# Products in eight small TensorE tiles in the last stages of a gated S4D and spectral mix

## The chip, the cores and the metric

The kernel runs on one core of a Trainium2 chip. The metric is device time in microseconds (us), the median of several executions. PE is TensorE (PEld its weight loads), DVE is VectorE, ACT is ScalarE, POOL is GpSimd, SP is SyncE.

## The reference

For an input `x` of 2048 rows (time) and 640 channels it computes a gate `g` per row and mixes two branches with it:

```
g = sigmoid((x * gate_w).sum(-1))
a = irfft(rfft(x^T, 2L) * rfft(K, 2L))[:L]^T + x * D_skip     # S4D: K from A, C, dt by exponentials
b = irfft2(rfft2(x) * (w_r + 1j * w_i))                        # spectral filter over rows and channels
out = g * a + (1 - g) * b
```

`K[d, l] = 2 Re sum_n C[d, n] exp(A[d, n] dt[d] l)`, with 128 states for each of the 640 channels.

## The kernel before

All transforms are products with tables on TensorE, in float32. The transform over 4096 points (2048 rows and as many zeros) is done in two stages, of 64 and of 64 points; channels are in four blocks `c` of 160.

- `phase_p` and `phase_b` make the kernel `K`: exponentials and sines on ACT, products on DVE and POOL, sums over the states on PE (`p_k`, L693, tiles of 128 rows and 32 columns), result in `k_d`.
- `phase_a` transforms `x`: `stage1` (L335, result `t1`) and `stage2` (L348), result in `u_d`. Beside it sums `x * gate_w` on PE; at its end DVE spreads the sums from PSUM into `T.gate` (L441), with one partition for each of 128 positions and 16 columns. The second half of `phase_a` takes the even frequencies through the spectral filter (lines 447 to 600: `fo`, `xx`, `mm`, `p_eo`, with `ue` loaded from `u_d`) and leaves the result in `s3e_d`.
- `phase_c` and `phase_d` transform `K` (`stage1` in `first`, `stage2` in `fronts`), multiply with `u_d` (`ma`, `mb`, `t2`: L795 to L801), transform back a first time (`backs`, `p_i`, L814) and store to `s3_d`.
- The last stages, also in `phase_d`, transform back a second time and mix. `last_e(c, a)` multiplies the rows from `s3e_d` (`t3e`, loaded by `load_e`) with the table `e3e` and scales with `1 - g` into `oe` (L876). `last_c(c, a)` multiplies the rows from `s3_d` (`t3`, loaded by `load_c`) with `e3`, scales with `g` and adds `oe` (for `c < 3` a multiply on DVE, L898, and an add on POOL, L899; for `c == 3` one instruction on DVE for each of the output rows, L896), and stores to `out`. `a` is 0 or 8: a group of `AG = 8` of the 16 columns of positions, so there are 8 groups of each kind. I call the work of one call a group.

In both, a group is cut into 3, 3 and 2 columns of 160 channels. Each piece takes two matmuls of 128 rows and 64 columns, one to each half of PSUM's partitions (`halved`, or the loop in `last_c`):

```
for i in (0, 64):
    nc.tensor.matmul(out[i:i + 64], w[:, i:i + 64], x, start=True, stop=True)
```

The tables hold zeros: `e3` has two copies of a 64 x 32 table on its diagonal, `e3e` has four of a 32 x 32 table.

The order is written out by hand. `merge` takes from several generators so that what they `yield`, divided by each stream's weight, grows together. In `phase_d`, for block `c` and `g` from 0 to 4, the streams are `mains` (`fronts` of one group of frequencies and `backs` of an earlier one, weight 4.8), `last_e(c, ...)` or `last_c(c - 1, ...)` (weight 2.4 each) and `first` of the next block (2.1). So `last_e(c)` runs in `g` 1 and 2 (2 and 3 for `c = 0`), `last_c(c - 1)` in `g` 3 and 4 for `c` 1 and 2; `last_c(2)` and `last_c(3)` run after the loop. `behind(T.mm)` sets the products behind the last matmul of `backs` on PE. [...]

Of the kernel before, what the change touches and what calls it, by code (L numbers as in the profile page):

```python
# [17 lines left out]
L = 2048  # L18
D = 640
# [31 lines left out]
def _tables():  # L51
# [11 lines left out]
    e1 = e1.reshape(2, 128, 128)  # L63

    kr = kr[:32].reshape(64, 32)
    e3 = np.zeros((64, 2, 2, 32))
    for j in range(2):
        e3[:, j, j, :] = kr

    e3e = np.zeros((32, 4, 4, 32))  # L70
    for r in range(4):
        e3e[:, r, JR[r], :] = kr[32:64]
    one = np.tile(np.eye(32), (4, 1))
    c1 = np.concatenate([
        e1[0], e1[1], e3.reshape(4, 32, 64).swapaxes(0, 1).reshape(128, 64), e3e.reshape(128, 128), np.eye(128), one,
        np.repeat([-1.0, 1.0], 64)[:, None], np.repeat([1.0, -1.0], 64)[:, None],
        np.full((128, 1), HALF_PI)], 1)

# [67 lines left out]


def _lay_back(y):
    y = y.reshape(4, 2, 2, 32, 16, 160)
    return np.ascontiguousarray(y.transpose(3, 2, 1, 4, 0, 5).reshape(1, L, D))  # L150


class Ctx:
    pass


def halved(nc, out, w, x):

    for i in (0, 64):
        nc.tensor.matmul(out[i:i + 64], w[:, i:i + 64], x, start=True, stop=True)  # L160


def merge(*streams):
# [20 lines left out]
def body(tc, A, out):  # L184
    nc = tc.nc
    T = Ctx()
    with ExitStack() as top:
        dram = top.enter_context(tc.tile_pool(name="dram", bufs=1, space=DRAM))
        T.u_d = dram.tile([4, 128, 17, 2, 160], F32, name="u_d")
        T.s3e_d = dram.tile([4, 32, 64, 160], F32, name="s3e_d")  # L190
        T.s3_d = dram.tile([4, 64, 64, 160], F32, name="s3_d")
        T.k_d = dram.tile([4, 128, 40, 64], F32, name="k_d")
        T.par_d = dram.tile([8, 16, 8, 5, N], F32, name="par_d")
        cst = top.enter_context(tc.tile_pool(name="cst", bufs=1))
        c1 = cst.tile([128, A["t_c1"].shape[1]], F32, name="c1")
# [10 lines left out]
        T.e3, T.e3e, T.id, T.one = take(64), take(128), take(128), take(32)  # L206
# [146 lines left out]
def phase_a(tc, A, T):  # L353
# [3 lines left out]
    with ExitStack() as ctx:  # L357
# [79 lines left out]
        V.tensor_reduce(out=lr[:, :], in_=lg.rearrange("p x a -> p a x"), axis=mybir.AxisListType.X, op=ALU.add)  # L437
        for r in range(4):
            P.matmul(p[32 * r:32 * r + 32, :], T.one, lr[:, :], start=True, stop=True)
        for r, x in enumerate((slice(31, 15, -1), slice(32, 48), slice(15, None, -1), slice(48, 64))):  # L440
            V.tensor_copy(T.gate[32 * r:32 * r + 32, 0, :], p[32 * r:32 * r + 32, x])  # L441


    with ExitStack() as ctx:
# [321 lines left out]
def phase_d(tc, A, T, ctx, out):  # L766
# [6 lines left out]
    o4 = ctx.enter_context(tc.tile_pool(name="d_o", reuse_waits="tile", bufs=4))  # L773
    dk = ctx.enter_context(tc.tile_pool(name="d_wk", reuse_waits="tile", bufs=1))
    o2 = ctx.enter_context(tc.tile_pool(name="d_o2", reuse_waits="tile", bufs=2))
    ps = ctx.enter_context(tc.tile_pool(name="c_ps", reuse_waits="tile", bufs=3, space=PSUM))
    pd = ctx.enter_context(tc.tile_pool(name="d_ps", reuse_waits="tile", bufs=2, space=PSUM))

    def load(c, g0, gn, st):
        nl = st.nl = 128 if g0 < 16 else 64  # L780
# [56 lines left out]
        while len(late) > (1 if i > 15 else 2):  # L837
            yield from backs(*late[0], sts.pop(late.pop(0)))

    def gate(i, a, n):  # L840
        return T.gate[:, i, a:a + n].unsqueeze(2).broadcast_to([128, n, 160])

    with tc.issue_after(T.trig.ins):
        S.activation(T.gate[:, 1, :], T.gate[:, 0, :], AF.Sigmoid, scale=-1.0)
# [6 lines left out]

    def load_e(c):
        t3es[c] = dk.tile([128, 16, 160], F32, tag="t3e", name="t3e")
        nc.sync.dma_start(t3es[c][:, :, :], T.s3e_d[c].rearrange("k (r a) d -> (k r) a d", r=4))

    def load_c(c, p, n, parts=1, eng=nc.sync):

# [4 lines left out]
        w = 16 // parts  # L862
        for y in range(p // 16, (p + n) // 16):
            src = T.s3_d[c, 16 * y:16 * y + 16].rearrange("k (j x a) d -> (k j) x a d", x=2, j=2)
            for a in range(0, 16, w):
                T.ld = eng.dma_start(t3s[c][y::4, :, a:a + w], src[:, :, a:a + w])

    def last_e(c, a):

        oe = oes[c, a] = o4.tile([128, AG, 160], F32, tag="oe", name="oe")  # L870
        for i in range(0, AG, 3):
            n = min(3, AG - i)
            p = pd.tile([128, 3, 160], F32, tag="pd", name="p_e")
            with behind(T.mm):
                halved(nc, p[:, 0:n], T.e3e, t3es[c][:, a + i:a + i + n])
            V.tensor_tensor(out=oe[:, i:i + n], in0=p[:, 0:n], in1=gate(1, a + i, n), op=ALU.mult)  # L876
            yield 0.8

    held = []

    def last_c(c, a):
# [6 lines left out]
        for i in range(0, AG, 3):  # L888
            n = min(3, AG - i)
            p = pd.tile([128, 3, 160], F32, tag="pd", name="p_c")  # L890
            with behind(T.mm):
                for x in range(2):
                    P.matmul(p[64 * x:64 * x + 64, 0:n], T.e3, t3[:, x, a + i:a + i + n], start=True, stop=True)  # L893
            if c == 3:
                for j in range(n):
                    V.scalar_tensor_tensor(out=ot[:, i + j], in0=p[:, j], scalar=T.gate[:, 0, a + i + j:a + i + j + 1], in1=oe[:, i + j], op0=ALU.mult, op1=ALU.add)  # L896
# [3 lines left out]
            if c < 2 and i + n == AG:  # L900
                G.dma_start(out[c, :, a:a + AG], ot[:, :, :])
            elif c == 3 and i + n > (5 if a else 6):
                x = i if a and i > 3 else 0
                nc.sync.dma_start(out[c, :, a + x:a + i + n], ot[:, x:i + n])
            yield 0.8
        if c == 2:
            held.append((out[c, :, a:a + AG], ot))

# [69 lines left out]
```

## Time and profile before

| | |
|---|---|
| median of 3 runs | 605.25 us (603.96 to 610.56) |
| profiled execution | 608.74 us, its span 607.0 us, granted clock 0.966 |
| PE busy | 535.8 us, 88% |
| DVE busy | 500.2 us, 82% |
| ACT busy | 364.8 us, 60% |
| POOL busy | 267.0 us, 44% |
| DMA | 101.98 MB, mean 168 GB/s |
| `p_e` (L160), `p_c` (L893) | 96 MATMUL records each |

Busy time is the time in which an engine had at least one instruction under way; the ends of matmuls are modelled. In the chain that ended last, each step goes back to what released it. In the view by stage, a row gives for each engine its busy time and number of instructions in that stretch. A window of the timeline merges instructions of one line that follow each other: start, length, count.

### The profile page before, as it was taken

The numbers are of one execution on the slowest core, as the hardware profiler recorded it, in microseconds if no ns is written. First come the engines' busy times: TensorE is split into PE (matmuls) and PEld (weight loads), VectorE is DVE, ScalarE is ACT, GpSimd is POOL, SyncE is SP. The second block draws the span as 40 slices with busy tenths as digits, with TensorE's granted clock in tenths as the row PEclk, the third lists the DMA queues.
The fourth block names the chain that finished last, engine by engine and source line by source line (L and its number), as shares of the span: only waits on it lengthen the run. The fifth ranks groups of instructions, "written<-read, shape, count | busy, mean of one in ns | idle before, by whom it ended". The sixth has DMA issues, their size and how long they took to land.

```text
span 607.0 us, 16654 instructions
## 1 busy us (share of the span) xinstructions
PE 535.8 (88%) x7084; PEld 405.6 (67%) x7084; DVE 500.2 (82%) x748; ACT 364.8 (60%) x659; POOL 267.0 (44%) x246
## 2 busy tenths in 40 slices
PE   9688979989968989989798999898989999999874
PEld 7576657766656657676566676565878877787631
DVE  5971597598899989999999899979399796987974
ACT  4556775576846876888589888799723332231210
POOL 4931252053525344454326335416254347547441
PEclk9899989989989996998899999999999999999998
DMA  8787204245612320332250233006685989889776
GB/s 341 293 288 268 79 5 151 69 154 181 239 43 67 97 87 13 108 118 109 67 151 12 75 97 110 24 28 200 224 346 184 356 273 299 291 271 310 225 231 239
DMA packets 48083, 101.98 MB, mean 168 GB/s; under 512 B 3316, under 2 KB 32776, under 8 KB 46248
## 3 DMA queue, kind: packets, MB, share of 16 engines
q1 hardware_dynamic: 24888, 67.74, 32.3%
q10 hardware_dynamic: 20080, 22.52, 11.9%
q0 software_dynamic: 3040, 10.65, 5.3%
q8 instruction: 56, 0.92, 0.6%
q14 instruction: 19, 0.16, 0.1%
HBM read 60.91 MB, written 39.98 MB: 166 GB/s over the span
## 4 chain that ended last, share of the span: by engine, by line
PE 51%; DVE 27%; ACT 9%; DMA 8%; issue 4%; POOL 1%; ACTq 0%; DVEq 0%; POOLq 0%; SPq 0%
PE p_eo L551 8%; PE p_s L348 8%; PE p_s L335 6%; PE p_e L638 5%; PE p_k L693 4%; PE p_i L814 4%; PE p_p L649 3%; DVE q L652 3%; PE p_d L518 2%; DVE t L801 2%; PE p_i L565 2%; PE p_t L502 2%; DVE ma L795 2%; PE p_c L893 2%; PE p_d L519 2%
## 5 line engine op out<-in xcount | busy, mean ns | idle before, releaser
L679 POOL TENSOR_TENSOR y<-e,sc 128x512 f32<-128x512 f32 x40 | 56.7, 1418 | 131.0 <-ACT sc L665 60.3
L348 PE MATMUL p_s<-t,w 128*64 128x160 f32 x1056 | 92.4, 314 | 10.2 <-ACT ut L382 5.1
L348 PEld LDWEIGHTS p_s<-t,w 128*64 128x64 f32 x1056 | 76.5, 139 | 21.4 <-ACT ut L382 6.0
L640 ACT ACTIVATE e<-p_e 128x512 f32<-128x512 f32 x120 | 68.6, 602 | 22.7 <-PE p_e L638 20.4
L551 PE MATMUL p_eo<-td,pmt 107*128 107x321 f32 x204 | 69.0, 459 | 3.9 <-ACT pmt L505 3.9
L693 PE MATMUL p_k<-x,y 128*32 128x64 f32 x2560 | 63.6, 229 | 9.8 <-DVE x L677 2.9
L693 PEld LDWEIGHTS p_k<-x,y 128*32 128x32 f32 x2560 | 46.1, 113 | 38.0 <-issue 29.4
L652 DVE SCALAR_TENSOR_TENSOR q<-q,p_p 128x512 f32<-128x512 f32 x80 | 53.4, 681 | 13.5 <-ACT q L651 11.8
L336 ACT COPY t<-p_s 128x512 f32<-128x512 f32 x40 | 24.6, 623 | 65.2 <-PE p_s L335 41.8
L638 PE MATMUL p_e<-rm,par 128*128 128x512 f32 x120 | 58.7, 519 | 3.4 <-ACT e L640 2.8
L680 POOL TENSOR_TENSOR y<-e,sc 128x512 f32<-128x512 f32 x40 | 54.5, 1362 | 6.5 <-ACT sc L666 6.5
L800 POOL TENSOR_TENSOR t<-ma 64x320 f32<-64x320 f32 x32 | 28.0, 875 | 61.4 <-DVE ma L795 51.8
L551 PEld LDWEIGHTS p_eo<-td,pmt 107*128 107x128 f32 x204 | 38.4, 198 | 19.6 <-ACT pmt L505 6.9
L677 DVE TENSOR_TENSOR x<-e,cx 128x1024 f32<-128x1024 f32 x40 | 48.6, 1214 | 2.2 <-ACT cx L668 2.2
L651 ACT ACTIVATE q<-p_p 128x512 f32<-128x512 f32 x80 | 46.5, 592 | 4.2 <-PE p_p L649 3.8
L649 PE MATMUL p_p<-rp,par 128*128 128x512 f32 x80 | 43.5, 548 | 4.5 <-DVE q L652 4.5
L814 PE MATMUL p_i<-t,w 128*64 128x160 f32 x528 | 42.7, 300 | 4.4 <-POOL t L801 3.4
L335 PE MATMUL p_s<-c,kt 128*64 128x128 f32 x640 | 43.0, 274 | 3.9 <-DVE mb L796 2.0
L335 PEld LDWEIGHTS p_s<-c,kt 128*64 128x64 f32 x640 | 38.0, 136 | 12.6 <-issue 7.7
L816 ACT COPY s<-p_i 128x640 f32<-128x640 f32 x32 | 21.8, 694 | 40.0 <-PE p_i L814 30.4
L335 PE MATMUL p_s<-c,u 128*64 128x128 f32 x640 | 41.5, 278 | 2.5 <-ACT ut L382 2.5
L795 DVE TENSOR_TENSOR ma<-p_s,us 128x640 f32<-128x640 f32 (+1 forms) x36 | 28.2, 784 | 18.8 <-PE p_s L348 11.5
(153 smaller groups left out, 1181.5 us busy)
## 6 DMA issues: line engine op xcount, KB each, us to landing
u_d<-ut SPq DMA_DIRECT2D x32, 320.0 KB, 2.6
us<-u_d ACTq DMA_DIRECT2D x16, 640.0 KB, 6.0
s_d<-s ACTq DMA_DIRECT2D x15, 640.0 KB, 8.3
t<-s_d SPq DMA_DIRECT2D x14, 640.0 KB, 5.9
ww<-in_w_l SPq DMA_DIRECT2D x8, 642.0 KB, 4.0
ue<-u_d SPq DMA_DIRECT2D x8, 640.0 KB, 4.4
k_d<-kt SPq DMA_DIRECT2D x4, 1280.0 KB, 7.6
kt<-k_d SPq DMA_DIRECT2D x8, 640.0 KB, 5.9
```

Source lines behind the costliest of these rows:

```text
L335: nc.tensor.matmul(p[64 * ri:64 * ri + 64, j, :], src(i + j), e1[ri], start=True, stop=True)
L348: ins = nc.tensor.matmul(p[64 * j:64 * j + 64, i, 160 * ri:160 * ri + 160], w2[:, x, 64 * ri:64 * ri + 64], t1[:, x // 2 if x < 32 else K0 ...
L551: P.matmul(p[:, :E], st.pmt[:DC, c, w, j, :], tv[:DC, w, c, :], start=c == 0, stop=c == 2)
L638: P.matmul(p[:, :], pars[t], rm[:, c:c + 512], start=True, stop=True)
L640: st.exp = S.activation(ef[:, c:c + 512], p[:, :], AF.Exp)
L649: P.matmul(p[:, :], pars[t], rp[:, c:c + 512], start=True, stop=True)
L652: V.scalar_tensor_tensor(out=qf[:, c:c + 512], in0=qf[:, c:c + 512], scalar=MAGIC, in1=p[:, :], op0=ALU.subtract, op1=ALU.subtract)
L677: V.tensor_tensor(out=x[:, 0].rearrange("p d (h j) -> p d h j", h=2), in0=e[:, :, 0:64].rearrange("p d (h j) -> p d h j", h=2), in1=cx.uns ...
L679: G.tensor_tensor(out=y[:, 1], in0=e[:, :, 64:96], in1=sc[:, 0], op=ALU.mult)
L680: G.tensor_tensor(out=y[:, 0], in0=e[:, :, 64:96], in1=sc[:, 1], op=ALU.mult)
L693: P.matmul(st.pb[32 * r:32 * r + 32, o, :], y[:, ri, 4 * qq + JR[r], :], x[:, ri, 4 * qq + JR[r], :], start=t % 2 + qq + 1 - ri == 0, stop ...
L814: T.mm = P.matmul(p[x:x + 64, i // 2, 160 * (i % 2):160 * (i % 2) + 160], T.w3[:, k0 + h + i, x:x + 64], t2[:, h + i, :], start=True, stop ...
```

## The change

The last stages use tiles of 64 rows (`last_c`) or 32 rows (`last_e`) and 32 columns. A product (`product`) is eight matmuls of 320 columns of data: four quarters of PSUM's partitions (`s`) by two halves of rows (`j`), each `j` into a bank of its own. Two products make a group. The tables lose their zeros: `e3` and `e3e` are 32 columns wide. The rows of `t3` are laid so that the two values of `j` lie in the two halves of the partitions, and inside each half every fourth partition belongs to one load; `load_c` and `load_e` read their sources in that order. Evacuation takes 640 elements at once (`four` picks four of a group's eight columns). The positions are spread differently over partitions and columns, so `T.gate` is filled by 16 copies instead of 4, and `_lay_back`, which undoes the layout on the host without arithmetic, changes. `pd` is gone; `ps` has four buffers. In `c == 3` the second group is stored in two halves of four columns.

```diff
-    e3 = np.zeros((64, 2, 2, 32))
-    for j in range(2):
-        e3[:, j, j, :] = kr
...
+    e3 = np.tile(kr.reshape(4, 16, 32).swapaxes(0, 1).reshape(64, 32), (2, 1))
+    e3e = np.tile(kr[32:64], (4, 1))
...
-        for r, x in enumerate((slice(31, 15, -1), slice(32, 48), slice(15, None, -1), slice(48, 64))):
-            V.tensor_copy(T.gate[32 * r:32 * r + 32, 0, :], p[32 * r:32 * r + 32, x])
+        for r in range(4):
+            o = slice(32 * r, 32 * r + 32)
+            g = T.gate[o, 0, :].rearrange("p (x j v) -> p x j v", x=2, j=2)
+            for x in range(2):
+                i = 16 * x + 4 * r
+                V.tensor_copy(g[:, x, 0], p[o, 31 - i:(27 - i if i < 28 else None):-1])
+                V.tensor_copy(g[:, x, 1], p[o, 32 + i:36 + i])
...
-    ps = ctx.enter_context(tc.tile_pool(name="c_ps", reuse_waits="tile", bufs=3, space=PSUM))
-    pd = ctx.enter_context(tc.tile_pool(name="d_ps", reuse_waits="tile", bufs=2, space=PSUM))
+    ps = ctx.enter_context(tc.tile_pool(name="c_ps", reuse_waits="tile", bufs=4, space=PSUM))
...
-        nc.sync.dma_start(t3es[c][:, :, :], T.s3e_d[c].rearrange("k (r a) d -> (k r) a d", r=4))
+        nc.sync.dma_start(t3es[c].rearrange("p a d -> p (a d)"), T.s3e_d[c].rearrange("k (r a) d -> r k (a d)", r=4))
...
-            src = T.s3_d[c, 16 * y:16 * y + 16].rearrange("k (j x a) d -> (k j) x a d", x=2, j=2)
-            for a in range(0, 16, w):
-                T.ld = eng.dma_start(t3s[c][y::4, :, a:a + w], src[:, :, a:a + w])
+            src = T.s3_d[c, 16 * y:16 * y + 16].rearrange("k (j a) d -> j k a d", j=2)
+            for a in range(0, 32, 32 // parts):
+                T.ld = eng.dma_start(t3s[c].rearrange("p x a d -> p (x a) d")[y::4, a:a + 32 // parts], src[:, :, a:a + 32 // parts])
+
+    def product(w, t, x, v, rows):
+        p = ps.tile([128, 2, 512], F32, tag="ps", name="p_l")
+        with behind(T.mm):
+            for s in range(4):
+                for j in range(2):
+                    r = slice(64 * j + rows[0], 64 * j + rows[1])
+                    P.matmul(p[32 * s:32 * s + 32, j, 0:320], w[r, :], t[r, 4 * s + v:4 * s + v + 2, :], start=True, stop=True)
+        return p[:, :, 0:320].rearrange("p j (v d) -> p j v d", v=2)
...
-        for i in range(0, AG, 3):
-            n = min(3, AG - i)
-            p = pd.tile([128, 3, 160], F32, tag="pd", name="p_e")
-            with behind(T.mm):
-                halved(nc, p[:, 0:n], T.e3e, t3es[c][:, a + i:a + i + n])
-            V.tensor_tensor(out=oe[:, i:i + n], in0=p[:, 0:n], in1=gate(1, a + i, n), op=ALU.mult)
-            yield 0.8
+        x = a // AG
+        for v in (0, 2):
+            p = product(T.e3e, t3es[c], x, v, (32 * x, 32 * x + 32))
+            V.tensor_tensor(out=four(oe, v), in0=p, in1=gate(1, a, v), op=ALU.mult)
+            yield 1.2
...
+            p = product(T.e3, t3[:, x], x, v, (0, 64))
...
-                V.tensor_tensor(out=ot[:, i:i + n], in0=p[:, 0:n], in1=gate(0, a + i, n), op=ALU.mult)
-                (V if c == 2 and a and n < 3 else G).tensor_tensor(out=ot[:, i:i + n], in0=ot[:, i:i + n], in1=oe[:, i:i + n], op=ALU.add)
+                V.tensor_tensor(out=four(ot, v), in0=p, in1=gate(0, a, v), op=ALU.mult)
+                (V if c == 2 and a and v else G).tensor_tensor(out=four(ot, v), in0=four(ot, v), in1=four(oe, v), op=ALU.add)
```

More of the change, by code (lines that the diff above doesn't have):

```diff
@@ L148, in _lay_back @@
 def _lay_back(y):
-    y = y.reshape(4, 2, 2, 32, 16, 160)
-    return np.ascontiguousarray(y.transpose(3, 2, 1, 4, 0, 5).reshape(1, L, D))
+    y = y.reshape(4, 4, 32, 2, 2, 4, 160)
+    return np.ascontiguousarray(y.transpose(2, 4, 3, 1, 5, 0, 6).reshape(1, L, D))
 class Ctx:
     pass
-def halved(nc, out, w, x):
-    for i in (0, 64):
-        nc.tensor.matmul(out[i:i + 64], w[:, i:i + 64], x, start=True, stop=True)
 def merge(*streams):
@@ L205, in body @@
         T.e1 = [take(128), take(128)]
-        T.e3, T.e3e, T.id, T.one = take(64), take(128), take(128), take(32)
+        T.e3, T.e3e, T.id, T.one = take(32), take(32), take(128), take(32)
         T.sg = [take(1), take(1)]
@@ L887, in last_c @@
             ot = up.tile([128, 4, 2, 160], F32, tag="us", name="ot").rearrange("p x y d -> p (x y) d")
[L888 to L893, printed above, removed]
+        x = a // AG
+        for v in (0, 2):
+            p = product(T.e3, t3[:, x], x, v, (0, 64))
             if c == 3:
-                for j in range(n):
-                    V.scalar_tensor_tensor(out=ot[:, i + j], in0=p[:, j], scalar=T.gate[:, 0, a + i + j:a + i + j + 1], in1=oe[:, i + j], op0=ALU.mult, op1=ALU.add)
-            else:
-                V.tensor_tensor(out=ot[:, i:i + n], in0=p[:, 0:n], in1=gate(0, a + i, n), op=ALU.mult)
-                (V if c == 2 and a and n < 3 else G).tensor_tensor(out=ot[:, i:i + n], in0=ot[:, i:i + n], in1=oe[:, i:i + n], op=ALU.add)
-            if c < 2 and i + n == AG:
+                for j in range(2):
+                    for i in range(v, v + 2):
+                        o = 4 * j + i
+                        V.scalar_tensor_tensor(out=ot[:, o], in0=p[:, j, i - v], scalar=T.gate[:, 0, a + o:a + o + 1], in1=oe[:, o], op0=ALU.mult, op1=ALU.add)
+            else:
+                V.tensor_tensor(out=four(ot, v), in0=p, in1=gate(0, a, v), op=ALU.mult)
+                (V if c == 2 and a and v else G).tensor_tensor(out=four(ot, v), in0=four(ot, v), in1=four(oe, v), op=ALU.add)
+            if c < 2 and v:
                 G.dma_start(out[c, :, a:a + AG], ot[:, :, :])
[L902 to L905, printed above, removed]
+            elif c == 3 and (v or a):
+                o = out[c, :, a:a + AG]
+                if a:
+                    nc.sync.dma_start(four(o, v), four(ot, v))
+                else:
+                    nc.sync.dma_start(o, ot[:, :, :])
+            yield 1.2
         if c == 2:
```

13 lines of the change are left out of this document (6 added, 7 removed).

## The prediction

> **What bounds the kernel now.** I read the page first (busy shares, then the chain that ended last), then busy time by stage, then the chain in order of time, and last single groups.
>
> ```profile
> PE 535.8 (88%) x7084; PEld 405.6 (67%) x7084; DVE 500.2 (82%) x748; ACT 364.8 (60%) x659; POOL 267.0 (44%) x246
> ...
> PE 51%; DVE 27%; ACT 9%; DMA 8%; issue 4%; POOL 1%; ACTq 0%; DVEq 0%; POOLq 0%; SPq 0%
> ```
>
> Half of the chain is TensorE (PE) and a quarter VectorE (DVE). Both are averages, so the view by stage comes next; its columns are the stretch, its length, and PE, PEld, DVE, ACT, POOL busy, granted clock, DMA share, GB/s.
>
> ```profile
> 474.00:488.00 14.00, 13.15 (x180) 11.11 (x175) 13.48 (x18) 4.01 (x7) 7.49 (x8) 1.00 0.97 327
> 488.00:503.00 15.00, 14.46 (x195) 12.78 (x197) 14.44 (x21) 4.30 (x7) 7.18 (x8) 1.00 0.89 294
> 503.00:514.00 11.00, 10.05 (x110) 7.44 (x108) 5.24 (x10) 3.37 (x6) 7.99 (x10) 1.00 0.94 289
> 514.00:526.00 12.00, 11.53 (x160) 9.72 (x155) 11.80 (x16) 3.19 (x5) 6.88 (x8) 1.00 1.00 343
> 526.00:543.00 17.00, 15.73 (x210) 13.57 (x212) 16.38 (x23) 5.44 (x10) 8.54 (x10) 1.00 0.78 249
> 543.00:552.00 9.00, 8.61 (x88) 5.80 (x88) 4.56 (x9) 2.42 (x4) 4.62 (x6) 1.00 0.93 293
> 560.00:577.00 17.00, 14.49 (x164) 11.01 (x160) 16.72 (x25) 3.67 (x6) 7.66 (x9) 1.00 0.72 227
> 577.00:596.00 19.00, 10.68 (x95) 6.03 (x96) 11.69 (x18) 2.46 (x5) 9.96 (x10) 1.00 0.75 219
> 596.00:607.00 11.00, 6.46 (x24) 1.67 (x21) 5.13 (x16) 0.00 (x0) 0.00 (x0) 0.83 0.65 258
> ```
>
> So the last 130 us have three kinds of stretch. In 474 to 503, 514 to 543 and 560 to 577 DVE is 96 to 98% busy and PE hardly less: these hold the even products `last_e`. In 503 to 514 and 543 to 552 DVE is half idle and PE 91 to 96% busy: these hold `last_c` of blocks 0 and 1. From 577 on neither is full, and the chain shows what ends last there (start, length, what):
>
> ```profile
> 577.86 8.84 DMA s_d<-s
> ...
> 588.68 2.91 DMA s_d<-s
> ...
> 591.65 3.75 DMA t<-s_d
> 595.40 0.41 issue
> 595.81 4.06 PE p_c L893 x12
> ...
> 603.25 0.29 DVEq L974
> ```
>
> From 577.86 to 595.40 it is store, store, load. `last_c` of block 2 runs under these transfers, so what it gains is worth nothing; `last_c` of block 3 follows the load, 595.8 to the end, and everything it gains counts.
>
> **The change part by part.** *Products on PE.* Each `matmul` of float32 leaves two MATMUL records (48 calls of L893 leave 96). How the time of a record goes with the number of tiles is in these rows, from the chain and from two stretches of PE's timeline:
>
> ```profile
> 399.11 0.54 PE p_eo L551 x2
> ...
> 488.54 1.03 PE p_e L160 x4
> ...
> 491.58 0.81 PE p_e L160 x4
> ...
> 494.35 0.54 PE p_e L160 x4
> ```
>
> ```profile
> 492.22 1.04 PE L335 MATMUL p_s<-c,kt 128*64 128x128 f32 x16
> 493.10 1.25 PE L814 MATMUL p_i<-t,w 128*64 128x160 f32 x16
> ```
>
> ```profile
> 434.15 0.50 PE L335 MATMUL p_s<-c,kt 128*64 128x128 f32 x6
> 434.57 1.10 PE L693 MATMUL p_k<-x,y 128*32 128x64 f32 x64
> 435.61 0.55 PE L335 MATMUL p_s<-c,kt 128*64 128x128 f32 x6
> ```
>
> One tile of full width: 0.54 us for 2 records of 321 columns, 0.84 ns a column. Two tiles of 64 columns (L335): 16 records of 128 in 493.10 - 492.22 = 0.88 us, 0.43 ns. Four tiles of 32 columns (L693): 64 records of 64 from 434.57 to 435.61, 1.04 us. In this row a change of tile shape hides as well: the 6 records of L335 ahead take 0.42 us (434.15 to 434.57) where three pairs at 0.11 make 0.33, so about 0.095 us goes with a change of shape; 1.04 less 0.095 over 64 is 14.8 ns, 0.23 ns a column. So 1, 2 and 4 tiles run at once, at 0.84, 0.43 and 0.23.
>
> Eight tiles are new: two halves of rows times four quarters of columns. If they go on as 1, 2, 4 did, a column costs about 0.115 ns; if the two halves of rows take turns, 0.23. The trace has no two row tiles in flight together. I take 0.115, as the row it is nearest to in kind (L693, four tiles with weights and data of their own) scales by 3.65 of 4, and keep 0.23. [...]
>
> A product is 16 records of 320 columns: 5120 x 0.115 = 0.59 us, and as the stages around it use 128x64 tiles, two changes of shape, 0.19: 0.78 us. A group (8 rows of output) has two: 1.56 us. Before it had 0.81 + 0.81 + 0.54 = 2.16 us by the rows above (1.03 holds some waiting). So 0.60 us of PE is saved a group, 9.6 us over 16 groups. What it is worth depends on the stretch. Four groups of `last_c` in the PE-bound stretches: 2.4 us; DMA stands at 0.93 there and ScalarE and GpSimd have their own order, so I count 2.0. Six groups of `last_e` in the DVE-bound stretches: DVE is idle 0.52 + 0.56 + 0.20 + 0.62 + 0.28 = 2.2 us there in all, which is the most that PE can give back; I count 0.7. Block 0's two `last_e` and block 2's `last_c`: 0.
>
> *Evacuation.* Three multiplies of 480, 480 and 320 become two of 640.
>
> ```profile
> L876 DVE TENSOR_TENSOR oe<-p_e,gate 128x480 f32<-128x480 f32 x16 | 10.5, 657 | 0.5
> L876 DVE TENSOR_TENSOR oe<-p_e,gate 128x320 f32<-128x320 f32 x8 | 3.8, 481 | 0.0
> L795 DVE TENSOR_TENSOR ma<-p_s,us 128x640 f32<-128x640 f32 x32 | 26.3, 822 | 18.8 <-PE p_s L348 11.5 <-issue 5.4 <-POOL t L801 1.4
> ```
>
> 2 x 657 + 481 = 1795 ns becomes 2 x 822 = 1644 (L795 has the same shape, one operand in PSUM): 0.15 us a group, on the path for the six groups where DVE is full: 0.9 at most, and less as instructions overlap at their ends; 0.5. GpSimd's adds keep their elements, and GpSimd is never full in the rows by stage: 0. In block 2 the last add, now 640 wide, moves to DVE under the final transfers: 0.
>
> *The last products.* Rows of the end:
>
> ```profile
> L896 DVE SCALAR_TENSOR_TENSOR ot<-p_c,gate,oe 128x160 f32<-128x160 f32 x16 | 5.1, 377 | 5.3 <-PE p_c L893 5.1
> ```
>
> ```profile
> 600.60 3.31 SPq L904 DMA_DIRECT2D out<-ot  x3
> 600.96 2.59 DVE L896 SCALAR_TENSOR_TENSOR ot<-p_c,gate,oe 128x160 f32<-128x160 f32 x8 [0.39 <-PE p_c L893]
> ```
>
> ```profile
> core 0: 607.0 us, clock 0.966
> ```
>
> Today PE paces DVE here (5.1 us of DVE's waiting, clock 0.83): the last of 16 multiply-adds ends at 603.55. After the change the first can start some 0.9 us after 595.81 (0.59 and the way out), then they run one behind the other, at 0.29 us (8 within 2.59 with one wait): 16 x 0.29 = 4.7 and four handovers of 0.08, so 601.7, 1.85 us earlier. PE stays ahead even at half the clock (1.18 us a product against 1.16 of DVE). The three output transfers, first issue 600.60, end with the span 6.4 us later; if they are what counts, the gain is the first issue's: 595.81 + 0.9 + 8 x 0.29 + 0.2 = 599.2, 1.4 us. The last transfer grows from 2 to 4 rows of output. I take 1.6; between 0 (four at once) and 1.9.
>
> *Gate copies.* This is the part that costs. `T.gate` is filled by 16 copies instead of 4, far from the last stages, and these rows show where:
>
> ```profile
> L441 DVE COPY gate<-p_g x4: 154/170/179, 152.9 to 153.5; 32x16 f32<-32x16 f32 x4
> ```
>
> ```profile
> 153.46 0.18 DVE gate L441
> ...
> 153.65 0.99 DVE fo L482
> ...
> 154.67 4.58 DMA ue<-u_d
> ```
>
> ```profile
> 160.00:180.00 20.00, 13.83 (x84) 11.78 (x82) 20.00 (x29) 10.91 (x20) 9.36 (x8) 0.91 0.34 128
> ```
>
> The copies are on the chain that ended last. Behind them on DVE stands L482, which frees `ue` for the load at 154.67, and behind that load DVE is busy without a gap for 20 us. A copy takes 0.17 us for 16 elements; by the two forms of L876 above an element costs 1.1 ns, so with 4 elements it takes nearly as long, and 12 more cost some 2.0 us. I count 1.6, as a later stretch where PE sets the pace may take some back; bounds 0.3 and 2.2.
>
> *Buffers and transfers.* Products now take their PSUM from one ring of four two-bank buffers instead of two single banks of their own beside a ring of three. Between two changes of block the ring serves 6 tiles of the main stages, or 8 with two products, so the distance back stays half a turn: 0, bounds -1 and +4.4 (what the products wait for DVE now, below, if it passed to the stages behind). Loads keep their sizes (32 rows of 20 KB, 128 of 10 KB), in another order of the source, and the one cut in two becomes 32 pieces of 10 KB instead of 64 of 5 KB: 0. The table loaded at the start is 64 KB smaller, of 102 MB in all: 0.
>
> *Sum*: -2.0 - 0.7 - 0.5 - 1.6 + 1.6 = -3.2 us. The profiled execution took 608.74 us (span 607.0 and 1.7 around it), 3.5 above the median of the three runs; 3.2 off the median, 605.25, is 602.0.
>
> **The rivals.** *A: the row halves take turns.* Then a product is 1.18 + 0.19 = 1.37 us and a group 2.74 instead of 2.16. The four PE-bound groups lose 2.4 us, the six others up to 3.6 in stretches where PE is nearly full already (say 2.5), the end gains nothing, at the half clock it loses some 0.8, and the copies cost 1.6, less 0.5 of evacuation: +6.8, 612.0 us. For it: nothing in the trace overlaps two row tiles. Against it: 1, 2 and 4 column tiles scale. Decides if a product takes over 1.0 us (two products and their changes then equal a group of before). This is also the case in which "eight at once" isn't so. *B: PE's gain is kept and DVE swallows the copies.* PE-bound groups 2.4, the DVE-bound ones all of the 2.2 us, evacuation 0.9, the end 1.9, copies 0.3: -7.1, 598.2. For it: while PE is 96% busy beside a full DVE, any release lets DVE run on. Against: a full DVE has nothing to run on to, and DMA reaches 1.00. *C: the shared ring stalls PE.*
>
> ```profile
> PEld p_e L160 <- DVE oe L876: 6.6, 7, 1.2
> PE p_e L160 <- DVE oe L876: 4.4, 5, 0.9
> ```
>
> Today a late evacuation holds back the next product alone. In one ring the stage behind it waits too, stage 1 among them, whose own evacuation is on the idle ScalarE. If each of the 28 products ahead of the end holds it for half a multiply, 0.4 us, that is 11 us on the forecast's -3.2 and 613.0. Against: the order of the rings' turns as above. *D: DMA sets the pace*, at 0.89 to 1.00 in 474 to 526: then the loops give nothing and only the end and the copies count, 605.3.
>
> **How the numbers follow.** Forecast 0.46, its own range 599.5 to 604.5 by the bounds of the counted parts; B 0.22, D 0.12, A 0.13, C 0.07. A measurement of this kernel can tell about 1% (599.2 to 611.3) from no change. Faster by over 1%: most of B (0.18) and the lower edge of the forecast (0.07), 0.25. Slower: half and more of A and C, 0.13. The rest, 0.62, is within 1%. The range takes in B, D and the forecast, and reaches towards A: 597.5 to 610.0.
>
> **What would show it.** Right: a product's 16 records within 0.6 us of each other's start and 0.1 us lost on either side; the stretch from the block's g=4 about 1 us shorter each; the first L896-like instruction within 1.0 us of the last load and 16 of them without waits over 0.15; 16 gate copies over some 2.8 us at 153, with the load behind them 2 us later. Wrong: records of the two row halves one after the other; stage 1 or stage 2 waiting on the products' evacuation for over 5 us in total; a chain from 577 to 595 that isn't store and load any more. If the 2 us at 153 are gone by 200, the copies cost nothing and B is nearer.

## The result, and the profile after

The changed kernel took 808.67 us in the median of 6 runs (803.27 to 811.96), the kernel before 609.62 beside it: a ratio of 1.3325 [1.3257, 1.3393]. The forecast was 602.0. The profiled execution took 805.83 us, with a span of 804.0. The engines' busy times and the two rows of the chain that ended last, from the page of the profile:

```profile
PE 546.3 (68%) x7404; PEld 414.9 (52%) x7404; DVE 497.2 (62%) x746; ACT 364.8 (45%) x659; POOL 264.6 (33%) x240
...
DMA 41%; PE 36%; DVE 12%; ACT 8%; issue 2%; ACTq 0%; POOL 0%; SPq 0%; DVEq 0%; POOLq 0%
DMA s_d<-s 23%; DMA t<-s_d 11%; PE p_eo L545 6%; PE p_s L324 5%; PE p_e L632 4%; DMA t3e<-s3e_d 4%; PE p_k L687 3%; PE p_s L337 3%; PE p_d L512 3%; DMA u_d<-ut 2%; PE p_d L513 2%; PE p_p L643 2%; PE p_i L559 2%; PE p_t L496 2%; DVE q L646 2%
```

The engines have about as much work as before: PE 546.3 us against 535.8, DVE 497.2 against 500.2. They wait. DMA has gone from 8% of the chain to 41%, and it is the transfers of the last stages: the stores to `s_d`, the loads `t` from it and the loads `t3e`. The chain's longest steps behind 430 us, in order of time (start, length, what):

```profile
439.11 28.22 DMA t3e<-s3e_d
485.49 35.89 DMA s_d<-s
...
542.37 31.30 DMA t<-s_d
...
630.65 30.70 DMA t<-s_d
...
719.26 37.80 DMA s_d<-s
...
772.76 23.82 DMA t<-s_d
```

Before, the longest of them was 8.84 us. A table by stage (stretch, length, PE, PEld, DVE, ACT, POOL busy, granted clock, DMA share, GB/s) shows two of these steps:

```profile
542.00:574.00 32.00, 0.13 (x8) 0.16 (x16) 0.00 (x0) 0.00 (x0) 0.00 (x0) 0.50 0.31 101
...
630.00:661.00 31.00, 0.00 (x0) 0.00 (x0) 0.00 (x0) 0.00 (x0) 0.00 (x0) 0.50 0.21 70
```

All five engines stand still for 31 us, and yet only 0.21 of 16 DMA engines are busy: 3.4 engines, 70 GB/s. Before, the same stages moved 219 to 343 GB/s at shares up to 1.00. So there is no lack of transfers; they are not spread. The granted clock stands at 0.50 there, with TensorE idle.

What SP waits for behind 430 us at the line that loads `t3` (line, what it waits for: us in total, times, longest), before and after:

```profile
SPq L866 <- DMA s_d<-s: 98.1, 15, 12.7
```

```profile
SPq L863 <- DMA s_d<-s: 198.3, 11, 37.6
```

A load waits for the stores of its rows before and after; the wait has doubled, though the stores are not changed: they are held back beside the loads. By the packet records, in the chain's step of 719.26, 373 and 533 of the stores' packets of 640 bytes start in the first two stretches of 2 us (719 to 723), and then, up to 753, 4 to 8 in each, beside 4 to 6 packets of 20,480 bytes of the loads. ACT, which issues them, is held up as well: the issue of one store took it 13.56 us (490.39 in its timeline), before at most 1.04. The DMA view of before and after (queue: packets, MB, share of 16 engines' span), before first:

```profile
q1 hardware_dynamic: 24888, 67.74, 32.3%
...
t<-s_d SPq DMA_DIRECT2D x14, 640.0 KB, 5.9
t3e<-s3e_d SPq DMA_DIRECT2D x4, 1280.0 KB, 9.0
```

```profile
q1 hardware_dynamic: 24808, 67.74, 24.5%
```

24.5% of 804.0 is 197 us, 32.3% of 607.0 is 196 us: the packets themselves took as long as before, on fewer engines at a time.

The products themselves came nearly as forecast. In the timeline of PE, a product:

```profile
474.82 0.77 PE L872 MATMUL p_l<-t3e,c 32*32 32x320 f32 x16
475.52 1.31 PE L807 MATMUL p_i<-t,w 128*64 128x160 f32 x16
```

16 records of 320 columns and their changes of shape take 475.52 - 474.82 = 0.70 us. Eight tiles do run at once: one after the other, at the 0.84 ns a column of a single tile, the 5120 columns would take 4.3 us.

### The profile page after: what moved, and what is told of

Read it like the earlier page. It is cut to its first block, busy times and chain, and to the rows that moved or that the text cites. A ratio compares the mean times of both kernels' runs of the same rounds, so it can differ in the third digit from the quotient of the medians.

```text
span 804.0 us, 17292 instructions
## 1 busy us (share of the span) xinstructions
PE 546.3 (68%) x7404; PEld 414.9 (52%) x7404; DVE 497.2 (62%) x746; ACT 364.8 (45%) x659; POOL 264.6 (33%) x240
## 3 DMA queue, kind: packets, MB, share of 16 engines
q1 hardware_dynamic: 24808, 67.74, 24.5%
## 4 chain that ended last, share of the span: by engine, by line
DMA 41%; PE 36%; DVE 12%; ACT 8%; issue 2%; ACTq 0%; POOL 0%; SPq 0%; DVEq 0%; POOLq 0%
DMA s_d<-s 23%; DMA t<-s_d 11%; PE p_eo L545 6%; PE p_s L324 5%; PE p_e L632 4%; DMA t3e<-s3e_d 4%; PE p_k L687 3%; PE p_s L337 3%; PE p_d L512 3%; DMA u_d<-ut 2%; PE p_d L513 2%; PE p_p L643 2%; PE p_i L559 2%; PE p_t L496 2%; DVE q L646 2%
## 5 line engine op out<-in xcount | busy, mean ns | idle before, releaser
L337 PE MATMUL p_s<-t,w 128*64 128x160 f32 x1056 | 98.2, 327 | 12.7 <-ACT ut L371 5.6
L872 PE MATMUL p_l<-t,c 64*32 64x320 f32 x256 | 17.1, 625 | 131.8 <-DMA t<-s_d 118.6
L337 PEld LDWEIGHTS p_s<-t,w 128*64 128x64 f32 x1056 | 80.8, 147 | 25.3 <-ACT ut L371 6.5
L872 PEld LDWEIGHTS p_l<-t,c 64*32 64x32 f32 x256 | 4.3, 131 | 140.1 <-issue 124.3
L902 DVE TENSOR_TENSOR ot<-p_l,gate 128x640 f32<-128x640 f32 x12 | 9.9, 822 | 105.5 <-PE p_l L872 105.5
L324 PE MATMUL p_s<-c,kt 128*64 128x128 f32 x640 | 48.0, 302 | 16.9 <-ACT s L809 14.8
L807 PE MATMUL p_i<-t,w 128*64 128x160 f32 x528 | 49.1, 337 | 13.4 <-ACT t L325 9.5
L324 PEld LDWEIGHTS p_s<-c,kt 128*64 128x64 f32 x640 | 41.8, 154 | 25.7 <-ACT s L809 17.5
L903 POOL TENSOR_TENSOR ot<-ot,oe 128x640 f32<-128x640 f32 x11 | 17.0, 1546 | 105.7 <-issue 88.2
L807 PEld LDWEIGHTS p_i<-t,w 128*64 128x64 f32 x528 | 40.7, 154 | 20.1 <-issue 14.9
```

The costliest lines, as they stand in the source:

```text
L324: nc.tensor.matmul(p[64 * ri:64 * ri + 64, j, :], src(i + j), e1[ri], start=True, stop=True)
L337: ins = nc.tensor.matmul(p[64 * j:64 * j + 64, i, 160 * ri:160 * ri + 160], w2[:, x, 64 * ri:64 * ri + 64], t1[:, x // 2 if x < 32 else K0 ...
L807: T.mm = P.matmul(p[x:x + 64, i // 2, 160 * (i % 2):160 * (i % 2) + 160], T.w3[:, k0 + h + i, x:x + 64], t2[:, h + i, :], start=True, stop ...
```

## The experiments

**The first four: how the loads are spread.** Theory 1: the order of the source's dimensions decides how many DMA engines share a load. After the change the outermost dimension is `j` (2) for `t3` and `r` (4) for `t3e`; before it was `(k j)`, 32, and `(k r)`, 128. Theory 2: the small tiles and the shared ring are slow. Theory 3: the order of the rows is slow in itself.

e1: the kernel after, each load cut along that dimension.

```diff
-        nc.sync.dma_start(t3es[c]..., T.s3e_d[c].rearrange("k (r a) d -> r k (a d)", r=4))
+        for r in range(4):
+            nc.sync.dma_start(t3es[c][32 * r:32 * r + 32]..., T.s3e_d[c].rearrange("k (r a) d -> r k (a d)", r=4)[r])
...
-                T.ld = eng.dma_start(t3s[c]...[y::4, a:a + 32 // parts], src[:, :, a:a + 32 // parts])
+                for j in range(2):
+                    T.ld = eng.dma_start(t3s[c]...[64 * j + y:64 * j + 64:4, a:a + 32 // parts], src[j, :, a:a + 32 // parts])
```

> Edit: the changed kernel, but each load of t3 is issued as two transfers, one for each half j (16 rows each), and each load of t3e as four, one for each r (32 rows each). Bytes, rows, places and everything else stay. Theory 1 (a load runs on only as many DMA engines as the outermost dimension of its source has entries: 2 for t3, 4 for t3e): t3 loads land in 4 to 7 us instead of 24 to 36, the waits for them go, and the kernel takes 598 to 608 us. Theory 2 (the small tiles, the shared PSUM ring or the new order of the work make it slow): it stays near 800. Theory 3 (reading the source in j-major order is slow in itself): it stays over 750, since the order is kept.

630.48 us, 1.0343 [1.0303, 1.0384]: above the 598 to 608 that theory 1 expected, but 178 of the 199 us are gone with no change to products, tables or order of rows. Theory 3, which keeps it over 750, falls. SP's wait for the stores, 198.3 us after the change, is 57.8. The loads in its DMA view (size, median us from issue to landing):

```profile
t<-s_d SPq DMA_DIRECT2D x28, 320.0 KB, 5.0
...
t3e<-s3e_d SPq DMA_DIRECT2D x16, 320.0 KB, 6.8
```

e2: the other way round, the products, tables, PSUM pools and gate of before, with rows laid and loaded as in after.

```diff
-        nc.sync.dma_start(t3es[c][:, :, :], T.s3e_d[c].rearrange("k (r a) d -> (k r) a d", r=4))
+        nc.sync.dma_start(t3es[c]..., T.s3e_d[c].rearrange("k (r a) d -> r k (a d)", r=4))
...
-            src = T.s3_d[c, 16 * y:16 * y + 16].rearrange("k (j x a) d -> (k j) x a d", x=2, j=2)
+            src = T.s3_d[c, 16 * y:16 * y + 16].rearrange("k (j a) d -> j k a d", j=2)
```

> Edit: the kernel before with its 128x64 tiles, its tables with zeros, its four gate copies and its PSUM pools; only the rows of t3 and t3e are laid as in the changed kernel, with the tables' rows permuted to match, so that the loads are the changed kernel's loads with an outermost dimension of 2 and 4 (the one load that is cut in two becomes four, as the two halves of x are apart). Theory 1: about 800 us (780 to 830), all of the loss from the loads alone. Theory 2: 605 to 612 us. Theory 3: about 800 as well, so this run tells 1 and 3 from 2, and the run with loads split by j tells 1 from 3.

812.1 us, 1.3349 [1.3296, 1.3401]: the whole loss, without one small tile. Its chain, by line, has the rows of after:

```profile
DMA s_d<-s 20%; PE p_eo L551 6%; DMA t<-s_d 5%; PE p_s L348 5%; PE p_s L335 4%; PE p_e L638 4%; DMA t3e<-s3e_d 4%; PE p_k L693 3%; DVE q L652 2%; PE p_i L565 2%; PE p_p L649 2%; PE p_t L502 2%; PE p_e L160 2%; DVE x L677 2%
```

Theory 2 falls, theory 1 stands. e3 and e4 do one half of e1's diff each: e3 only the loads of `t3` (its last two added lines), e4 only those of `t3e` (its first two).

> Edit: the changed kernel with only the loads of t3 split by j; t3e is still loaded with an outermost dimension of 4. Theory 1: the four t3e loads still take about 28 us each; the first of them is on the path (28 us in the chain of the changed kernel) and the others delay the transfers queued behind them on the same four engines: 640 to 690 us. Theory 2: near 800.

> Edit: the changed kernel with only the loads of t3e split by r; t3 is still loaded with an outermost dimension of 2. Theory 1: the t3 loads on two engines, 17 of them of some 25 to 31 us each as those engines take one after the other, stay the pace: 17 x 640 KB on two engines that move about 21 GB/s together is 510 us less what overlaps with nothing else needed; 740 to 790 us. Theory 2: near 800.

e3 took 676.17 us, 1.112 [1.1063, 1.1176]; e4 777.11, 1.278 [1.2714, 1.2845]. Either load alone costs; `t3` on two engines is the worse. (Both lie where theory 1 had them. In e4's expectation, though, 21 GB/s is what the trace gives for one engine, 70 GB/s over 3.4, and not for two together, so its range was met partly by luck.) Theory 1 also gives the length of the steps. At 630.07, 630.65 and 631.18 two loads of `t3` and one of `t3e` were issued. If the same two engines carry both loads of `t3` and their part of `t3e`, each has 32 packets of 20,480 bytes and 32 of 10,240; at the 776 and 386 ns that the packet records of the kernel before have in the median, that makes 37 us. The chain shows 30.70 for the second load of `t3`; the rest falls to `t3e`. The packet records of this stretch bear it out: from 642 to 653 us a mean of 2.01 packets of 20,480 bytes and 2.02 of 10,240 are under way. So both loads of `t3` share the same two engines. (From 425 us on, one or two packets of 20,480 bytes are under way in 209.0 of the 209.5 us in which any is; before, it is up to 17.) The last packet of the two loads ends at 660.9, the last of `t3e` at 672.6, 41 us behind the first packet at 631.4.

**e5 to e8: what the rest is.** e1 still lost 3.4%. e5 is the kernel after with the load sources of before, in one transfer each:

```diff
-        nc.sync.dma_start(t3es[c]..., T.s3e_d[c].rearrange("k (r a) d -> r k (a d)", r=4))
+        nc.sync.dma_start(t3es[c][:, :, :], T.s3e_d[c].rearrange("k (r a) d -> (k r) a d", r=4))
...
-            src = T.s3_d[c, 16 * y:16 * y + 16].rearrange("k (j a) d -> j k a d", j=2)
+            src = T.s3_d[c, 16 * y:16 * y + 16].rearrange("k (j a) d -> (k j) a d", j=2)
```

> Edit: the changed kernel with the sources of its loads in the order of before, (k j) and (k r), so that each load is one transfer of 32 or 128 rows again; the rows land on partitions that the tables do not expect, so the mixed result is made from permuted rows, with the same amount of work. Nothing else differs from the change. What was left when each load was split by j (1.034 of before) is either the number of transfers or the products. Theory 1a (twice and four times as many transfers make SP wait before it may issue): with the old number of transfers this takes 598 to 606 us, the forecast of the prediction with its loads at nothing. Theory 2 (small tiles, ring of four PSUM buffers): it stays at 620 to 630 us.

606.89 us, 0.9988 [0.9943, 1.0032]. In e5 the rows land where the tables don't expect them, so its output is not the right one; it serves for the time alone, with the same bytes and the same number of instructions. Its instructions stand on PE, DVE and POOL in the same order as those of after, so this is the loads alone, and it is also what the rest of the change is worth. e6 gives the products of before the pieces of e1, that is e2 with e1's diff:

> Edit: the kernel before, products and PSUM pools unchanged, with rows laid as in the changed kernel and each load split into two (t3) or four (t3e) transfers, so that each has 16 or 32 rows. Theory 1a: the transfers' number alone costs what was left: 625 to 635 us. Theory 2: 605 to 612 us, as neither small tiles nor the one ring are in it.

631.6 us, 1.0351 [1.0259, 1.0444], without small tiles and the one ring: the rest, too, belongs to the loads. e7 tried fewer pieces (32 `k` of one `j` in a transfer, `t3e` as before with tiles of 128 rows), e8 the same with the 16 gate copies replaced by 16 small matmuls and one copy.

```diff
+        for j in range(2):
+            q = 64 * j + 2 * (p % 32) + p // 32
+            T.ld = eng.dma_start(t3s[c]...[q:q + 2 * n - 1:2], T.s3_d[c, p:p + n, 32 * j:32 * j + 32].rearrange("k a d -> k (a d)"))
...
-            p = product(T.e3e, t3es[c], x, v, (32 * x, 32 * x + 32))
+            p = product(T.e3e, t3es[c], x, v, None)
```

> Edit: the changed kernel, but a t3 load now takes 32 rows k of one j (a single step in DRAM, every second partition in one half), so blocks 0 to 2 have as many t3 transfers as before the change, and block 3 two for each 16 k; t3e is loaded as before the change in one transfer, and its products use four tiles of 128x32 with zeros, eight matmuls as in the change. Right result. Theory 1a: 598 to 608 us: 5 more transfers than before instead of 29 more, some 0.35 us of PE more per even group, which DVE covers. Theory 2: 618 to 632 us.

The further edit of e8:

```diff
-                V.tensor_copy(g[:, x, 0], p[o, 31 - i:(27 - i if i < 28 else None):-1])
+                P.matmul(pv[o, x, 0], T.one, lr[:, 31 - i:(27 - i if i < 28 else None):-1], start=True, stop=True)
...
+        V.tensor_copy(T.gate[:, 0, :], p[:, 0:16])
```

> Edit: as the run with one j a load, and T.gate is filled by 16 small matmuls (4 columns each) and one copy instead of 4 matmuls and 16 copies. In the changed kernel the 16 copies took 1.57 us of DVE at 153 us against 0.73 before. If that is on the path, this is 0.8 to 1.5 us faster than the run with one j a load; if later stretches swallow it, no difference, within 0.5 us.

e7 took 625.31 us, 1.0276 [1.0201, 1.0352], where 598 to 608 was expected: a miss. A load now needs two stores and comes late (first load of `t3` issued at 481.52, before at 464.23), which may be a part of it; what this costs was not measured alone. e8 took 627.2, 1.0302 [1.024, 1.0363]. The two intervals overlap, so a gain of 0.8 to 1.5 us from taking the copies away can neither be seen nor excluded.

**e9 to e12: number or shape of the pieces.** I had put the rest down to the number of transfers (theory 1a). e9 has as many as e1 and e6, but cuts the loads of before by columns; e10 is the kernel after with the loads of `t3` as in e1 and `t3e` as in e7. The edit of e9 at `t3` (that at `t3e` takes 4 of the 16 columns at a time):

```diff
+                for x in range(2):
-                T.ld = eng.dma_start(t3s[c][y::4, :, a:a + w], src[:, :, a:a + w])
+                    T.ld = eng.dma_start(t3s[c][y::4, x, a:a + w], src[:, x, a:a + w])
```

> The kernel before with its own layout (32 rows a load of t3, 128 of t3e), but each transfer cut by columns: a t3 load in 2, a t3e load in 4. The number of transfers is that of e1 and e6 (29 more), each of them starting on 32 or 128 rows where e1 and e6 have 16 or 32. Theory 1a (the number of transfers costs the 3.4%, as a transfer waits for an older one on its semaphore): as e1 and e6, 625 to 635 us, ratio 1.03 to 1.04, with SP waiting on us<-u_d at the loads' lines, which before shows nowhere. Rival 1b (a load of 16 rows of 20 KB is slow in itself, whatever the number): 604 to 612 us, ratio 0.99 to 1.005.

> The kernel after with each t3 load in two transfers of 16 rows, as in e1, and t3e as before in one transfer of 128 rows, its products by tiles of 128 rows with zeros (four at once). 17 more transfers than before in place of e1's 29; products of last_e at four tiles cost about 0.6 us more each. Theory 1a, the number of transfers: about 17/29 of e1's loss, 1.02, 618 to 622 us with the slower products at most 2 more. Rival 1b, the loads of 16 rows alone: as e1, 628 to 632. If it is the four transfers of t3e at the start of a block that cost, 605 to 612.

e9: 607.33 us, 0.9992 [0.9947, 1.0037]. Theory 1a falls: 29 more transfers cost nothing, in the order that the build gave them. e10: 618.3, 1.0168 [1.008, 1.0256], where theory 1a had put it, but not for its reason, as e9 shows. So it is what the pieces are like. e11 keeps the layout of before and cuts by rows into lower and upper half, with an unbroken source; e12 has the broken source of e6, landing over the whole height.

```diff
+                for j in (0, 64):
+                    T.ld = eng.dma_start(t3s[c][j + y:j + 64:4, :, a:a + w], src[j // 4:j // 4 + 16, :, a:a + w])
```

```diff
+                for j in range(2):
+                    T.ld = eng.dma_start(t3s[c][y + 4 * j::8, :, a:a + w], src[j, :, :, a:a + w])
```

> The kernel before with its own layout, each load of t3 cut by rows in 2 (the first 16 rows to every fourth partition of the lower half, the other 16 to the upper half) and each load of t3e cut in 4 (32 neighbouring partitions each). The source of every piece is one unbroken stretch of 320 KB. As many transfers as in e6, e1 and e9. Theory 4 (e9 having shown that the number is free): a piece that lands in half or a quarter of the partitions moves more slowly, since all 16 engines write there at once; in e6 a packet of 20,480 bytes took 1251 ns in the median and one of 10,240 747, in the kernel before 776 and 386. Then 625 to 635 us here, ratio 1.03 to 1.04, and packets of about 1200 and 700 ns. Rival 5 (the broken source, every second or fourth row of the DRAM tile, is what is slow): 604 to 612 us, ratio 0.99 to 1.005, packets of 776 and 386 ns.

> The kernel before with its own layout, each load of t3 cut by j in 2 and each load of t3e by r in 4, so that the sources are exactly those of e6 (rows of 20 KB or 10 KB, 40 KB apart), but the rows land over the whole height: every eighth partition for t3, every fourth for t3e. As many transfers as in e6, e1, e9 and e11. Theory 4 (the partitions that a piece lands in): 604 to 612 us, ratio 0.99 to 1.005, packets of 20,480 and 10,240 bytes at about 776 and 386 ns. Rival 5 (the broken source): 625 to 635 us, ratio 1.03 to 1.04, packets of about 1200 and 700 ns.

e11 636.71 us, 1.0499 [1.0435, 1.0563]; e12 633.22, 1.0427 [1.0377, 1.0476]. Both are slow, e12 against theory 4, which had 604 to 612, so times alone don't tell theory 4 from rival 5. The packets do. Median ns of a packet on queue q1 behind 425 us; those of 20,480 bytes are loads of `t3`, most of those of 10,240 are of `t3e`:

| | 20,480 B | 10,240 B | `t3` lands on | `t3e` lands on |
|---|---|---|---|---|
| before | 776 | 386 | every 4th of 128 | 128 |
| after | 761 | 386 | every 4th of 128 (2 engines) | 128 (4 engines) |
| e6 | 1251 | 747 | every 4th of a half | 32 neighbours |
| e11 | 1094 | 688 | every 4th of a half | 32 neighbours |
| e12 | 1338 | 385 | every 8th of 128 | every 4th of 128 |
| e10, e16 | 1176, 1196 | 385, 388 | every 4th of a half | 128 |
| e7, e17 | 1446, 1473 | 385, 386 | every 2nd of a half | 128 |

A broken source is fast in e12's `t3e`, an unbroken one slow in e11: rival 5 falls. 32 neighbours or one half are slow, whatever the source: theory 4, except for e12's `t3`, which lands over the whole height and is slow. So the height alone does not sort the rows of the table; the pattern of partitions does. A packet of 20,480 bytes took 761 to 776 ns on every fourth of 128, 1094 to 1473 on a half and 1338 on every eighth of 128; one of 10,240 bytes took 385 to 388 on all 128 or on every fourth, and 688 to 747 on 32 neighbours. Why every eighth partition is slow, and why the slow rows differ among themselves, no run shows.

**e13 to e16: the order of instructions.** The build puts instructions in an order by its own estimate of the transfers, and e6, e11 and e12 all stand in one order, another than that of before. Theory O: that order is what costs. So I held every engine's instructions in a given order by edges of order alone, the loads of e13, e14, e15 and e16 being those of e6, e9, e1 and e10:

```diff
+    for v in json.loads(zlib.decompress(base64.b85decode(ORDER))).values():
+        for a, b in zip(v, v[1:]):
+            tc.add_manual_dep(at["I-%d" % b], "I-%d" % a, ...)
```

> The transfers and products of e6 (before's products, rows laid as in after, each load of t3 in 2 pieces of 16 rows, each of t3e in 4 of 32), but every engine's instructions held in the order that they have in the kernel before, the pieces of a load standing one behind the other at the load's place. Theory O (the order that the build chose for e6 is what cost it 3.5%): 603 to 612 us, ratio 0.995 to 1.005, though the packets stay slow. Theory P (pieces that land in half or a quarter of the partitions are slow): 625 to 635 us as e6, ratio 1.03 to 1.04.

> The transfers of e9 (cut by columns; 0.9992 in its own order) with every engine's instructions held in the order of e12 (1.043). Theory O: 625 to 640 us, ratio 1.03 to 1.05. Theory P: 603 to 612 us, as e9.

> e1, that is the kernel after with split loads, with every engine's instructions held in the order of e5 (whose order on PE, DVE and POOL is that of after). Theory O: as e5, 602 to 610 us, ratio 0.99 to 1.003; at the lower end it beats the kernel before. Theory P: 625 to 632 us, as e1.

> e10 (t3 in 2 pieces by j, t3e in one transfer with tiles of 128 rows) with every engine's instructions held in the order of e5. 17 more transfers than before in place of 29. Theory O: 603 to 611 us, ratio 0.99 to 1.005. Theory P: as e10, 616 to 620 us, ratio 1.017.

e13: 627.67 us, 1.0354 [1.0288, 1.0421], in the order of before as slow as e6 in its own (1.0351). e15: 627.0, 1.0311 [1.0245, 1.0378]; e16: 616.0, 1.0166 [1.0116, 1.0217]. Theory O falls as the cause. But e14, fast pieces in the order of e12, took 621.66, 1.0246 [1.018, 1.0311], between what the two theories had, where e9 with the same pieces was at 0.9992: an order made for other transfers costs these pieces 2.5%, so a part of e12's loss may be its order.

**e17: the partitions alone.** Theory 6: the partitions that a load of `t3` reaches set the time of its packets and cost time by themselves; packets then come near e7's 1446 ns and the kernel takes 1.01 to 1.025 of before, 613 to 624 us. The kernel before with as many transfers, the same sources and the same order on every engine; the 32 rows of a load of `t3` land on every second partition of one half.

```diff
-                T.ld = eng.dma_start(t3s[c][y::4, :, a:a + w], src[:, :, a:a + w])
+                T.ld = eng.dma_start(t3s[c][64 * (y // 2) + y % 2:64 * (y // 2) + 64:2, :, a:a + w], src[:, :, a:a + w])
```

> The kernel before, with as many transfers as it has, the same sources of 32 rows and the same order on every engine; only the 32 rows of a load of t3 land on every second partition of one half in place of every fourth of all, and the rows of the table e3 are permuted to match. [...] Rival 7 (it is the piece of 16 rows, one packet an engine, that is slow): 603 to 612 us, ratio 0.995 to 1.005, packets of about 776 ns.

610.75 us, 1.007 [1.0036, 1.0104]. The packets are as theory 6 has them, 1473 ns, the time is below its 1.01 to 1.025. Its DMA view, beside the rows of before above:

```profile
q1 hardware_dynamic: 24888, 67.74, 33.8%
...
t<-s_d SPq DMA_DIRECT2D x14, 640.0 KB, 7.1
```

The same packets and bytes took 33.8% of 608.4, 206 us of 16 engines, in place of 196, and a load 7.1 us in place of 5.9. So the partitions cost time by themselves, 0.7% here, and the number costs none by itself (e9). Pieces confined to half of the partitions and more of them together cost 1.7% (`t3` alone, e10 and e16, where the products of `last_e` at four tiles are in it too) to 3.5% (both, e6 and e13). What they add to each other is not settled. One thing is seen in such runs: SP's waits of e13 from 420 to 640 us hold loads that have nothing to do with SP's own:

```profile
SPq L869 <- DMA us<-u_d: 12.5, 2, 6.9
SPq L855 <- DMA us<-u_d: 12.0, 4, 6.3
```

24.5 us at the load lines; before has none, e9 7.8 at its own (in an execution of 614.93 us). The transfers of SP and ACT take turns on eight semaphores in the trace (in that of before 99, 101 to 103, 105 to 107 and 109), and the wait fits a transfer that is held until the one before it on its semaphore, here a load of `us` by ACT, has landed. That slow pieces and more of them make this wait long is an argument; no run takes it away alone.

No version beat the kernel before: e5, at 0.9988, bounds what the small tiles could bring with loads as fast as before. Another layout of `s_d` in DRAM, by which such loads would have both halves and 32 rows in their outermost dimension, wasn't tried.

## Why the prediction was wrong

The step that failed is under *Buffers and transfers*: "Loads keep their sizes (32 rows of 20 KB, 128 of 10 KB), in another order of the source, and the one cut in two becomes 32 pieces of 10 KB instead of 64 of 5 KB: 0." It should have been about 200 us: e2, with this order of the source and none of the rest, took 812.1 us, and e5, with all of the rest, 606.89. I compared bytes and rows and took the order of a source's dimensions for free. It is not a rival that came true either: D had DMA set the pace at the shares of before, but here the shares, 0.65 to 1.00 in the stages from 474 on, fell to 0.18 to 0.49 in those from 450 on, and the time rose, because two or four engines carried what 16 had.

The trace of after shows it: two packets of 20,480 bytes under way with two loads of `t3`, where before it was up to 17; four or fewer of 10,240 bytes in 98.6% of the time from 446 to 466 us, with one load of `t3e`, where before it was up to 17 too; 3.4 busy engines with all three under way (630 to 661 us); and 31 us where before a load took 5.9.

The other steps, by e5 and the traces:

*Products on PE.* 0.70 us a product with its changes of shape; taken was 0.78. Rival A (halves that take turns, 1.37) is out. TensorE was busy 529.0 us in e5 in place of 535.8, and the time did not show it.

*Evacuation.* By group and shape, e5:

```profile
L881 DVE TENSOR_TENSOR oe<-p_l,gate 128x640 f32<-128x640 f32 x16 | 13.2, 825 | 0.5
```

825 ns; taken was 822.

*The last products.* The chain of e5:

```profile
593.15 3.19 DMA t<-s_d
596.34 0.25 issue
596.58 1.39 PE p_l L872 x16
...
598.00 3.30 DVE ot L900 x11
```

The timeline of DVE has the last of the 16 multiply-adds end 4.76 us behind 598.00. From the load's landing that is 602.76 - 596.34 = 6.42 us; before it was 603.55 - 595.40 = 8.15. A gain of 1.7; taken was 1.6, between 1.85 by the prediction's working to this same point and 1.4 by the output transfers behind it. The parts of the 1.85 were off in ways that nearly cancel, which is luck: the first multiply-add began 1.42 us behind the first matmul and not 0.9, as that product took 1.39 us at a granted clock of 0.66 (596 to 607), and the 16 then took 4.76 us and not 5.0. Nor does the prediction's PE stay ahead at half the clock by its own numbers, 1.18 us against 1.16.

*Gate copies.* DVE's timeline after:

```profile
152.83 0.14 DVE L434 COPY gate<-p_g 32x4 f32<-32x4 f32 x1
152.90 0.14 DVE L435 COPY gate<-p_g 32x4 f32<-32x4 f32 x1
...
154.23 0.16 DVE L435 COPY gate<-p_g 32x4 f32<-32x4 f32 x1
154.40 0.83 DVE L476 TENSOR_TENSOR fo<-ue 128x640 f32<-128x640 f32 x1
```

A copy is shown with 0.14 us, but the next starts 0.07 to 0.17 later: 1.57 us in all, 0.84 more than the 0.73 of before. I had added whole durations, said 2.0 and counted 1.6. In the kernel after, the chain that ended last holds no copy: from 145 to 175 us it runs over PE and ACT. Whether 0.84 us counts in e5 is open, as e8 against e7 can't tell so little.

*Ring and sum.* Rival C (the shared ring stalls PE, 613.0) is out: e5 has the ring and lies at 606.89, and in it `stage1` and `stage2` on PE wait 1.3 us in all for the evacuation of `oe` (their weight loads 2.1). Without the loads the forecast was -3.2 us; e5's interval is -3.5 to +1.9 us, so the sum is neither shown nor excluded, nor is D's 0 (605.3); B's -7.1 lies outside.

## What to carry to other kernels

When a change reorders the dimensions of a transfer, read off the outermost one of its source before anything else: here 2 and 4 confined the loads to as many engines (3.4 busy of 16 with both kinds under way), and stores that had not changed waited with them (up to 37.80 us in the chain, before at most 8.84). Then look at which partitions the rows land on: packets of 20,480 bytes took 1094 to 1473 ns on a half and 1338 on every eighth partition, though that spans the whole height, against 761 to 776 on every fourth; those of 10,240 bytes took 688 to 747 on 32 neighbours against 385 to 388. Where all engines idle beside a transfer and DMA's share is low, as 0.21 here, ask whether the transfers are spread over the engines before counting them.

## What the hardware showed that I had not expected

- Loads on two and four engines held back stores that had not changed: `s_d<-s` steps of up to 36 and 38 us in the chain, before at most 8.84.
- Packets of 20,480 bytes took 776 ns where a load landed on every fourth of all partitions, and 1094 to 1473 where it landed on a half or on every eighth; of 10,240 bytes 386 against 688 to 747 where it landed on 32 neighbours.
- 29 more transfers that reach every fourth or every one of the 128 partitions cost nothing (0.9992 [0.9947, 1.0037]), while the same transfers in an order that the build made for others cost 2.5%.
- A change of tile shape and eight tiles of 320 columns: 0.70 us for 5120 columns, 0.14 ns a column with the changes in it.
